# A cross network on one core: row products of the middle layers in 32x32 pieces instead of 32x128

## The chip, the cores and the metric

One NeuronCore of a Trainium2 chip runs the whole program. The metric is the device time of one execution in microseconds; the runs of the kernel before have a median of 131.04 us (130.76 to 131.1).

Names used below: PE is TensorE, which multiplies (PEld its weight loads), ACT is ScalarE, DVE is VectorE, POOL is GpSimd, SP the engine that issues most DMAs. SBUF is the memory on the core, PSUM the eight banks (each 512 fp32 wide on 128 partitions) into which PE writes.

## The reference

Six layers of a cross network on a batch of 4096 rows of 416 features, all in bf16:

```python
B, F, D, L = 4096, 26, 16, 6
Din = min(F * D, 1024)          # 416
...
def reference(x0, ws, bs):
    x = x0
    for l in range(ws.shape[0]):
        x = x0 * (x @ ws[l] + bs[l]) + x
    return x
```

## The kernel before

**Layout.** The activations are kept transposed: features on partitions, batch rows along the free dimension. 416 features are three chunks of 128 (tiles `XM`, main part) and a remainder of 32. The remainder has only 32 features, so four groups of 512 batch rows are put below each other on the 128 partitions (tile `XR`: partitions 32g to 32g+31 hold group g). The batch is cut in two halves s of 2048 columns, each in four groups g of 512 columns (`CW`). `WM` holds the weights of the 384 main input features, `WR` those of the 32 remainder features, once on each strip of 32 partitions, so that group g finds them beside its data. `XM` and `XR` each have three buffers: x0, and two that the layers use in turn.

**A middle layer** (the loop over `l` from 1 to 4) has six tiles (s, m): for a half s and an output chunk m of 128 features, all four groups. A tile fills two pairs of banks (`new_pts`), one bank for a group. Its product is the sum of two parts:

- `mm_full` (L205), for each group: over the three input chunks k, and for each k four products of 128 input rows x 32 output columns, side by side in the array by columns (position (0, 32q)); 48 products for a tile.
- `mm_row` (L211), once for a tile: for each group g one product of 32 input rows x 128 output columns, the four side by side in the array by rows (position (32g, 0)), each into the bank of its group; 4 products for a tile.

The tiles are taken in pairs (ta, tb). Within a pair the order is fixed by the program: the `mm_full` of ta in all groups, then `mm_row` of ta (which closes its sums), `mm_row` of tb (which opens its sums), then the `mm_full` of tb. So the two `mm_row` calls stand next to each other; such a place is called a visit below. There are 4 layers x 3 pairs = 12 visits of 8 products. After the first pair of a layer `rem_pair` makes the 32 remainder outputs, in products of 128x32 (L217, L222).

**Behind the products.** `ew_main` takes a pair of banks (half h of a tile): ACT adds the bias and writes bf16 (L169), DVE multiplies by x0 (L179) and adds the layer's input (L180). In `ew_rem` the same is done for the remainder (L193, L198, L199). The order of instructions on every engine is the order in which the program is written; semaphores between the engines are put in from the tiles that each instruction reads and writes.

**The first layer** uses products of 128x128 (L240) and 32x128 (L247). **The last layer** turns the roles around, so that its output has batch rows on partitions: products of 128x128 (L357) and 32x128 (L366, and L371 for the bias), then ACT copies (L383, L396), DVE multiplies (L384, L397) and adds (L385, L400), and SP sends the result out.

Of the kernel before, what the change touches and what calls it, by code (L numbers as in the profile page):

```python
# [16 lines left out]
def kernel(  # L17
# [7 lines left out]
    nc = tc.nc  # L25
# [8 lines left out]
    CW = 512  # L34
# [19 lines left out]
    WR = const.tile([P, L, D], BF16)  # L54
# [146 lines left out]
    def mm_full(l, s, m, g, pts, cur, first, last):  # L201
        c0 = col0(s, g)
        for k in range(NK):
            for q in range(4):
                nc.tensor.matmul(pts[g // 2][32 * q:32 * q + 32, g % 2, :], lhsT=WM[:, l, k, 128 * m + 32 * q:128 * m + 32 * q + 32],  # L205
                                 rhs=cur[:, k, c0:c0 + CW], start=(first and k == 0), stop=(last and k == NK - 1),
                                 tile_position=(0, 32 * q), skip_group_check=True)

    def mm_row(l, s, m, pts, curR, first, last):
        for g in range(NG):  # L210
            nc.tensor.matmul(pts[g // 2][:, g % 2, :], lhsT=WR[32 * g:32 * g + 32, l, 128 * m:128 * m + 128],  # L211
                             rhs=curR[32 * g:32 * g + 32, CW * s:CW * s + CW],
                             start=first, stop=last, tile_position=(32 * g, 0), skip_group_check=True)

    def mm_rem(l, s, pr, cur, curR):
        for g in range(NG):
# [97 lines left out]
    cur, curR = XM[1], XR[1]  # L314
    for l in range(1, LL):
        nxt, nxtR = XM[1 + (l % 2)], XR[1 + (l % 2)]
        feeds_last = (l == LL - 1)
        tiles = [(s, m) for s in range(NS) for m in range(NK)]
        pts = {}

        def finish(t):
            s, m = t
            for h in range(2):
                ew_main(l, s, m, h, pts[t][h], cur, nxt)
            if feeds_last:
                xl_dmat(s, m, nxt)

        for n in range(0, len(tiles), 2):
            ta, tb = tiles[n], tiles[n + 1]
            pts[ta] = new_pts()  # L330
            for g in range(NG):
                mm_full(l, ta[0], ta[1], g, pts[ta], cur, True, False)
            mm_row(l, ta[0], ta[1], pts[ta], curR, False, True)
            pts[tb] = new_pts()
            mm_row(l, tb[0], tb[1], pts[tb], curR, True, False)
            finish(ta)
            for g in range(NG):
                mm_full(l, tb[0], tb[1], g, pts[tb], cur, False, True)
            finish(tb)
            if n == 0:  # L340
                rem_pair(l, cur, curR, nxtR, feeds_last)
        cur, curR = nxt, nxtR

    l = LL
# [111 lines left out]
```

## Time and profile before

| what | value |
|---|---|
| median of three runs | 131.04 us |
| the profiled execution | 130.19 us |
| its span, first to last instruction | 128.1 us |
| granted TensorE clock | 1.000 |
| middle layers on PE (first to last visit) | 28.4 to 99.6 us |
| products of L205, L211, all on PE | 1152, 96, 1677 |

How to read it. A line of a group gives the source line, engine, operation, output <- inputs and shape, then the number of instructions, busy time in us, the mean of one in ns, and the idle time of the engine just before them with what ended it. For a matmul, 128*32 stands for input rows x output columns of the array; 128x512 is the streamed operand. A line of the order of time gives the start in us, the length of the stretch, and what ran in it; matmuls of one kind are put together. Matmuls are pipelined: the record of one lasts 379 ns where the next ones start earlier, so the distance between starts, not the length of a record, says how fast they go. A line of waits gives who waited for whom, the sum in us, how often, and the longest. "issue" is time in which the engine waited for nothing that the profile shows.

### The profile page before, as it was taken

To read this page: it belongs to the slowest core of one execution; us is meant where nothing else is said; L and a number is where in the kernel's file an instruction comes from. 1 tells how busy PE (TensorE), PEld (TensorE's weight loads), DVE (VectorE), ACT (ScalarE), POOL (GpSimd) and SP (SyncE) were. 2 spreads that over 40 slices of the span, in tenths; PEclk is the share of its full clock that TensorE was granted. 3 is DMA by queue.
4 is the path that set the end of the run, shared out by engine and by line. 5 is a ranking of instruction groups with operands and counts; after the bars stand their busy time and mean duration, and the time that the engine had idled before them with its cause. 6 is when DMAs were issued, how large, how long until landed. Compare 5 with 4: busy or idle time off the path is not lost. (4 is left out here: it accounts for less than half of the span.)

```text
span 128.1 us, 3929 instructions
## 1 busy us (share of the span) xinstructions
PE 122.7 (96%) x1677; PEld 54.7 (43%) x1677; DVE 105.2 (82%) x192; ACT 83.5 (65%) x94; POOL 8.6 (7%) x29
## 2 busy tenths in 40 slices
PE   6999999999999999999999999999999999999960
PEld 3344344444444444444444544444444445445420
DVE  3347959357979898989898989898989999999991
ACT  2117559489666849666849666749666777567860
POOL 4282000120000000000000000000000300000000
PEclk9999999999999999999999999999999999999999
DMA  3999999999990000000000000000398899986663
GB/s 91 259 157 192 207 187 263 229 329 332 336 314 24 5 0 8 0 0 5 0 5 0 5 0 5 0 0 5 69 140 177 167 122 246 192 283 216 210 225 103
DMA packets 42029, 16.36 MB, mean 128 GB/s; under 512 B 30838, under 2 KB 42012, under 8 KB 42012
## 3 DMA queue, kind: packets, MB, share of 16 engines
q1 hardware_dynamic: 40512, 15.70, 55.0%
q10 hardware_dynamic: 1500, 0.42, 1.6%
q8 instruction: 13, 0.21, 0.7%
q14 instruction: 4, 0.03, 0.1%
HBM read 6.15 MB, written 3.41 MB: 75 GB/s over the span
## 5 line engine op out<-in xcount | busy, mean ns | idle before, releaser
L169 ACT ACTIVATE t<-PS,bM 128x1024 bf16<-128x1024 f32 x56 | 58.1, 1115 | 21.2 <-PE PS L211 21.2
L205 PE MATMUL PS<-XM,WM 128*32 128x512 bf16 x1152 | 65.2, 379 | 0.0
L205 PEld LDWEIGHTS <-WM 128*32 128x32 bf16 x1152 | 29.8, 97 | 33.7 <-issue 5.1
L179 DVE TENSOR_TENSOR t<-t,XM 128x1024 bf16<-128x1024 bf16 x48 | 33.4, 695 | 4.1 <-ACT t L169 4.1
L180 DVE TENSOR_TENSOR XM<-t,XM 128x1024 bf16<-128x1024 bf16 x48 | 33.5, 699 | 3.1
L357 PE MATMUL PS<-WM,XM 128*128 128x416 bf16 x96 | 17.9, 340 | 0.0
L240 PE MATMUL PS<-XM,WM 128*128 128x512 bf16 x72 | 16.5, 383 | 0.1
L383 ACT CAST t<-PS 128x832 bf16<-128x832 f32 x12 | 10.2, 852 | 5.0 <-PE PS L357 2.5
L357 PEld LDWEIGHTS <-XM 128*128 128x128 bf16 x96 | 8.9, 98 | 8.7 <-issue 2.1
L240 PEld LDWEIGHTS <-WM 128*128 128x128 bf16 x72 | 6.9, 99 | 9.4 <-issue 2.1
L222 PE MATMUL PS<-XM,WM 128*32 128x512 bf16 x120 | 8.2, 379 | 0.0
L193 ACT ACTIVATE t<-PS,bR 128x512 bf16<-128x512 f32 x10 | 6.8, 694 | 1.9 <-POOL WD L133 1.9
L385 DVE TENSOR_TENSOR o<-t,XLrows 128x832 bf16<-128x832 bf16 x12 | 7.1, 592 | 0.5
L211 PE MATMUL PS<-XR,WR 32*128 32x512 bf16 x96 | 7.3, 379 | 0.0
L384 DVE TENSOR_TENSOR t<-t,X0rows 128x832 bf16<-128x832 bf16 x12 | 7.0, 586 | 0.0
L300 POOL COPY XLrows<-scrR 128x512 bf16<-128x512 bf16 x2 | 1.4, 698 | 72.7 <-DMA scrR<-XR 72.7
L177 DVE TENSOR_TENSOR XM<-t,XM 128x1024 bf16<-128x1024 bf16 x7 | 4.7, 690 | 1.5 <-ACT t L169 1.4
L150 PE MATMUL PS<-warm 128*128 128x512 bf16 (+2 forms) x13 | 4.6, 536 | 1.0 <-DVE warm L87 1.0
L186 ACT ACTIVATE t<-PS,bM 128x512 bf16<-128x512 f32 x4 | 2.6, 685 | 3.8 <-PE PS L247 3.8
L162 ACT COPY XR<-xrt 64x256 bf16<-64x256 bf16 x2 | 1.2, 621 | 5.7 <-DVE xrt L161 5.7
L161 DVE STREAM_TRANSPOSE xrt<-xrem 64x256 bf16<-64x256 bf16 (+1 forms) x5 | 2.2, 477 | 3.2 <-DMA xrem<-in_x_dram 3.2
L396 ACT CAST t<-PS 128x416 bf16<-128x416 f32 x8 | 4.0, 506 | 1.0 <-PE PS L357 0.8
(44 smaller groups left out, 54.4 us busy)
## 6 DMA issues: line engine op xcount, KB each, us to landing
X0rows<-in_x_dram SPq DMA_DIRECT2D x8, 416.0 KB, 7.5
WM<-in_ws_dram SPq DMA_DIRECT2D x5, 312.0 KB, 6.7
out_dram<-o SPq DMA_DIRECT2D x3, 416.0 KB, 3.2
out_dram<-o SPq DMA_DIRECT2D x6, 208.0 KB, 2.5
out_dram<-o SPq DMA_DIRECT2D x8, 104.0 KB, 1.7
WR<-in_ws_dram SPq DMA_DIRECT2D x4, 130.0 KB, 5.7
WM<-in_ws_dram ACTq DMA_DIRECT2D x1, 312.0 KB, 3.4
XM<-in_x_dram SPq DMA_TRANSPOSE x8, 4.8
```

Source lines behind the costliest of these rows:

```text
L169: nc.scalar.activation(t[:], pt.rearrange("p a b -> p (a b)"), ACT.Identity, bias=bM[:, m, l:l + 1], scale=1.0)
L179: nc.vector.tensor_tensor(out=t, in0=t, in1=x0c, op=ALU.mult)
L180: nc.vector.tensor_tensor(out=nxt[:, m, c0:c0 + 2 * CW], in0=t, in1=cur[:, m, c0:c0 + 2 * CW], op=ALU.add)
L193: nc.scalar.activation(tr[:, 0:CW], pr, ACT.Identity, bias=bR[:, l:l + 1], scale=1.0)
L205: nc.tensor.matmul(pts[g // 2][32 * q:32 * q + 32, g % 2, :], lhsT=WM[:, l, k, 128 * m + 32 * q:128 * m + 32 * q + 32], rhs=cur[:, k, c0:c ...
L211: nc.tensor.matmul(pts[g // 2][:, g % 2, :], lhsT=WR[32 * g:32 * g + 32, l, 128 * m:128 * m + 128], rhs=curR[32 * g:32 * g + 32, CW * s:CW ...
L222: nc.tensor.matmul(pr[32 * g:32 * g + 32, :], lhsT=WM[:, l, k, NK * P:D], rhs=cur[:, k, c0:c0 + CW], start=False, stop=(k == NK - 1), tile ...
L240: nc.tensor.matmul(pt[:, gl, :], lhsT=WM[:, 0, k, 128 * m:128 * m + 128], rhs=cur[:, k, c0:c0 + CW], start=(first and k == 0), stop=(last ...
L357: nc.tensor.matmul(py[g // 2][:, g % 2, 0:D], lhsT=cur[:, k, q_cols(q, g)], rhs=WM[:, l, k, :], start=(first and k == 0), stop=((not first ...
L383: nc.scalar.copy(tv, py[h][:, :, 0:D])
L384: nc.vector.tensor_tensor(out=tv, in0=tv, in1=X0rows[:, b0:b0 + 5:4, :], op=ALU.mult)
L385: nc.vector.tensor_tensor(out=o, in0=tv, in1=XLrows[:, b0:b0 + 5:4, :], op=ALU.add)
```

## The change

In `mm_row` each product of 32x128 is issued as four products of 32x32: the 128 output columns are cut into four strips q of 32, each with its own 32 columns of `WR`, its own 32 partitions of the bank, and the array position (32g, 32q). The data streamed, the bank and the accumulation flags are as before. A visit then has 32 products instead of 8.

```diff
     def mm_row(l, s, m, pts, curR, first, last):
         for g in range(NG):
-            nc.tensor.matmul(pts[g // 2][:, g % 2, :], lhsT=WR[32 * g:32 * g + 32, l, 128 * m:128 * m + 128],
-                             rhs=curR[32 * g:32 * g + 32, CW * s:CW * s + CW],
-                             start=first, stop=last, tile_position=(32 * g, 0), skip_group_check=True)
+            for q in range(4):
+                nc.tensor.matmul(pts[g // 2][32 * q:32 * q + 32, g % 2, :],
+                                 lhsT=WR[32 * g:32 * g + 32, l, 128 * m + 32 * q:128 * m + 32 * q + 32],
+                                 rhs=curR[32 * g:32 * g + 32, CW * s:CW * s + CW],
+                                 start=first, stop=last, tile_position=(32 * g, 32 * q), skip_group_check=True)
```

## The prediction

> **What bounds the kernel now.** I read the page's busy line first, then the waits, then the middle layers' order of time, and the vector engine (DVE) up to the end.
>
> ```profile
> PE 122.7 (96%) x1677; PEld 54.7 (43%) x1677; DVE 105.2 (82%) x192; ACT 83.5 (65%) x94; POOL 8.6 (7%) x29
> ...
> L205 PE MATMUL PS<-XM,WM 128*32 128x512 bf16 x1152 | 65.2, 379 | 0.0
> ...
> L211 PE MATMUL PS<-XR,WR 32*128 32x512 bf16 x96 | 7.3, 379 | 0.0
> ```
>
> The matmul rows have no idle time before them. Busy alone says little for pipelined matmuls, so the waits decide:
>
> ```profile
> ACT t L169 <- PE PS L211: 21.2, 12, 2.2
> ...
> PEld L211 <- issue: 5.1, 12, 0.4
> PEld L205 <- issue: 5.1, 12, 0.4
> DVE t L179 <- ACT t L169: 4.1, 11, 0.9
> ```
>
> ScalarE (ACT) waits at all twelve visits for the row products of L211, and DVE waits for ACT at eleven of them: in the middle layers TensorE (PE) sets the pace. The order of time of PE shows one period, in waves of products that run side by side:
>
> ```profile
> 36.00 0.61 PE L211 MATMUL PS<-XR,WR 32*128 32x512 bf16 x8
> 36.54 5.36 PE L205 MATMUL PS<-XM,WM 128*32 128x512 bf16 x96
> 41.84 0.61 PE L211 MATMUL PS<-XR,WR 32*128 32x512 bf16 x8
> 42.38 5.36 PE L205 MATMUL PS<-XM,WM 128*32 128x512 bf16 x96
> ```
>
> From 36.54 to 41.84 are 5.30 us for 24 waves of four 128x32 products. The records of single products inside it lie 0.2155 us apart from wave to wave, and 24 x 0.2155 = 5.17. The other 0.13 us, and what a visit costs beyond two waves, is seen at its borders:
>
> ```profile
> 35.68 0.39 PE L205 MATMUL PS<-XM,WM 128*32 128x512 bf16 x4
> 36.00 0.39 PE L211 MATMUL PS<-XR,WR 32*128 32x512 bf16 x4
> ...
> 36.01 0.60 PE L211 MATMUL PS<-XR,WR 32*128 32x512 bf16 x6
> ...
> 36.54 0.40 PE L205 MATMUL PS<-XM,WM 128*32 128x512 bf16 x4
> ...
> 36.00 0.12 PEld L211 LDWEIGHTS <-WR 32*128 32x128 bf16 x8 [0.42 <-issue]
> ```
>
> The last wave of 128x32 starts at 35.68, the first of 32x128 at 36.00: 0.32 instead of 0.2155, so going over costs about 0.10. The second row wave starts at 36.23, 0.227 after the first, the next 128x32 wave at 36.54, 0.31 later: another 0.10 back. The weight loads, elsewhere a wave ahead, wait these 0.42 us for "issue": nothing is loaded ahead across the border. A visit, 36.00 to 36.54, is 0.54 us.
>
> Last, the end. DVE's order of time shows its last wait:
>
> ```profile
> 94.64 0.43 DVE L199 TENSOR_TENSOR XR<-t,XR 128x512 bf16<-128x512 bf16 x1
> 95.29 0.69 DVE L179 TENSOR_TENSOR t<-t,XM 128x1024 bf16<-128x1024 bf16 x1 [0.22 <-ACT t L169]
> 96.01 0.69 DVE L180 TENSOR_TENSOR XM<-t,XM 128x1024 bf16<-128x1024 bf16 x1
> ```
>
> Behind 95.29 no wait of DVE is listed up to 125.1: the end hangs on DVE from there. That operation follows the eleventh visit (93.71). The twelfth (99.55) has room: ACT's output for it is ready at 101.1 (99.98 plus one activation of 1.115), DVE takes it up at 101.49. So what ten visits and the first wave of an eleventh gain or lose goes into the end.
>
> **The change, part by part.** Twelve visits (four layers, three pairs of tiles) have 96 products of 32x128; they become 384 of 32x32. PE gets 288 matmuls and 288 weight loads more, 1677 to 1965 each; nothing else changes kind, place or order, and no DMA is added.
>
> *Array time.* Four strips by rows, with 512 columns streamed, were one wave; four by rows and four by columns are still one wave of 512, if all sixteen run together. Each direction alone does it now: four column strips start within 0.011 us (L205 above, x4 in 0.39 with 0.379 each), four row strips too. Both at once is in no row. Lower bound 0; upper bound, if the column strips of a row strip took turns, 3 more waves of 0.2155 for each of two: 1.29 us a visit. I take 0: it is the product of two things that the rows show, and each pair of strips has its own partitions and each g its own bank (pts[g // 2], g % 2).
>
> *Issue.* The four row products of a wave start at 36.000, 36.003, 36.007 and 36.010, their loads between them: 3.4 ns per load and product. Sixteen spread over 15 x 3.4 = 51 ns instead of 10. A product of wave two follows the one of wave one on its own strip, so the spread is carried on, not doubled; and the next 128x32 wave waits for the last one to be out, as it does now (302 ns from the last record of the row wave, 36.236, to the first load at 36.538). That is 12 x 3.4 = 41 ns a visit: 0.58 instead of 0.54. It could be hidden only where the border did not wait for the last product, bound 0; the upper bound is the slowest pace at which PE is seen fed, four loads and products in 0.2155, 54 ns each. I take 3.4, the row of the same line and place. The Trainium skill (TensorE: Matmul & The Clock Gate, section "Measured speedup vs the span model") counts about 4 ns of issue per tile; by it the added spread is 48 ns a visit and the sum below 0.50 instead of 0.43, an estimate.
>
> *Weight loads.* Sixteen in place of four, each shorter in columns: 128x32 loads take 97 ns, 32x128 loads 92, so no shorter by these rows. The first sixteen lie in the spread already counted; the second sixteen need about 16 x 3.4 = 54 ns of issue, then 97, inside the 216 ns of wave one: 65 ns of cover. Without it each further pair costs its 3.4.
>
> *Borders.* 128x32 to 32x32 takes the place of 128x32 to 32x128. Rows of other changes of shape:
>
> ```profile
> 102.47 0.39 PE L205 MATMUL PS<-XM,WM 128*32 128x512 bf16 x4
> 102.79 0.35 PE L357 MATMUL PS<-WM,XM 128*128 128x416 bf16 x1
> ...
> 103.68 0.34 PE L357 MATMUL PS<-WM,XM 128*128 128x416 bf16 x1
> 103.95 0.35 PE L366 MATMUL PS<-WR,XR 32*128 32x416 bf16 x4
> ```
>
> Columns alone (128x32 to 128x128): 0.32 instead of 0.2155. Rows alone (128x128 to 32x128): 0.27 instead of 0.175 from product to product there. Both at once (L205 to L211): 0.32. All are 0.10 over a wave, so the new one, rows alone, is taken at the same 0.10: change 0. Bounds: minus 0.10 on each side, if it needs no emptying; plus nothing the rows suggest.
>
> *Semaphores.* ACT's first half needs the products of g 0 and 1: eight issues instead of two, 6 x 3.4 = 20 ns later in the visit. That is all of the eleventh visit that DVE sees.
>
> *Sum.* 10 x 41 + 20 = 430 ns. PE itself ends its middle layers 12 x 41 = 0.49 us later; the last 0.06 lies in the 0.4 us of room. The profiled execution took 130.19 us (span 128.1), which becomes 130.62; the runs' median is 131.04, 0.85 above it, and I put the sum on that: 131.47, said as 131.5.
>
> **Rivals.**
> *PE is not fed fast enough.* The 3.4 ns are seen for bursts of at most some dozen instructions (four loads with four products and four further loads at 36.00); a visit now wants 64 in a row. If loads and products come every r ns, the point is r = 215.5/16 = 13.5. Up to there the spread grows (15 r); beyond, first to last product of a visit takes 31 r, against 0.236 now. At 13.5 that is 0.42, +0.18 a visit, x 10.5 = +1.9: 132.9. At 54, the seen floor of supply, 1.67: +15.1, 146. For it: nothing in the rows shows a longer burst. Against: loads run a wave ahead in L205, so there are instructions waiting, and the 0.42 us at each border refill what stands ahead. I price it at 13.5, since that is the geometric middle of 3.4 and 54: 133. The same page of the Trainium skill (section "Wait — 56ns, not 53.3ns?") states a floor of about 25 ns from start to start however small a product is; applied to sixteen strips it would give 31 x 25 = 0.78 a visit and some 136.7, an estimate; the 3.4 ns between strips here speak against it.
>
> *Column strips of one row strip take turns* (the change doesn't do what it says): 1.29 us a visit, x 10.5 to 12 = 13.5 to 15.5, about 145. Against: both directions work alone.
>
> *The border gets cheaper, and the kernel faster.* The place is the two borders of a visit; the new form keeps the 32 columns of its neighbours, so PE may load ahead across it and need no emptying. Price: 2 x 0.10 saved, 0.04 of spread lost: minus 0.16 a visit, x 10.5 = minus 1.7: 129.3. It decides as soon as the two borders together fall by more than 41 ns. DVE would follow: it waits 4.1 us in all there. Against: rows alone and columns alone each cost the full 0.10 elsewhere.
>
> **How the numbers follow.** 0.3%, 0.39 us, is about what a measurement of this kernel can tell from no change. Forecast (+0.3 to +0.6) 0.62, of it two thirds over 0.39; too slow a supply 0.17; turns 0.05; a cheaper border 0.12; a spread that is hidden (131.0) 0.04. Slower: 0.41 + 0.17 + 0.05 = 0.63. Same: 0.21 + 0.04 = 0.25. Faster: 0.12. The range 130.9 to 133.2 holds the forecast, the hidden spread and the supply up to a little past its point; the cheaper border, the turns and a far slower supply are left out, 0.2 together. The forecast's own range is 131.3 to 131.7.
>
> **What would show it.** The row group reads 32*32, x384. Right: its first to second wave still about 0.23, each visit about 0.58 from the first row product to the next 128x32 wave, sixteen starts within about 0.05, borders of 0.32, DVE's last wait still behind the eleventh visit and some 0.4 us later. A visit of 0.7 or more with even gaps of over 13 ns is the supply; one of 1.8 with groups of four 0.2155 apart is turns; weight loads of L211 no longer waiting for "issue" and a visit under 0.5 is the cheaper border. I am wrong if the borders or the gap between strips in the combined form differ from the rows of the single forms.

## The result, and the profile after

The changed kernel takes 131.5 us (131.1 to 132.01, 14 runs), the kernel before, on the same chips, 131.18 us (130.57 to 131.44, 14 runs). The ratio is 1.003, with a 95% interval of 1.0018 to 1.0043: slower by 0.39 us, 0.24 to 0.56 (0.32 between the two medians). The prediction had 131.5 and +0.43.

The group of the row products, and the waits, on the page and in the list of waits of the changed kernel:

```profile
PE 123.8 (96%) x1965; PEld 55.8 (43%) x1965; DVE 105.2 (81%) x192; ACT 83.5 (64%) x94; POOL 9.2 (7%) x29
...
L213 PE MATMUL PS<-XR,WR 32*32 32x512 bf16 x384 | 7.8, 379 | 0.0
...
ACT t L169 <- PE PS L213: 21.7, 12, 2.3
PEld L213 <- issue: 5.1, 12, 0.4
PEld L205 <- issue: 4.6, 12, 0.4
```

384 products of 32x32 take 7.8 us of busy time, where 96 of 32x128 took 7.3. The weight loads still wait 0.4 us for "issue" at each of the twelve visits: nothing is loaded ahead across the border. The order of time of PE around one visit:

```profile
36.54 0.39 PE L205 MATMUL PS<-XM,WM 128*32 128x512 bf16 x4
36.86 0.43 PE L213 MATMUL PS<-XR,WR 32*32 32x512 bf16 x16
...
37.09 0.42 PE L213 MATMUL PS<-XR,WR 32*32 32x512 bf16 x16
37.44 0.40 PE L205 MATMUL PS<-XM,WM 128*32 128x512 bf16 x4
...
36.86 0.20 PEld L213 LDWEIGHTS <-WR 32*32 32x32 bf16 x32 [0.42 <-issue]
```

Sixteen products start within 0.43 minus 0.384 (one record) = 0.05 us; the second wave starts 0.23 behind the first; the visit, 36.86 to 37.44, is 0.58. The single records give more digits. Over the twelve visits the mean is 0.5806 against 0.5404. The way in, from the last main product to the first row product, is 0.309 (before 0.312), the way out 0.304 (0.304).

The spans of the two profiled executions differ by more, 129.5 against 128.1. Most of that is not the change: the first visit starts at 29.26 instead of 28.44, and nothing ahead of it was edited. The eight kernels below, which share this unedited first layer, begin their first visit between 28.74 and 29.32. From the first visit to the last instruction it is 100.22 against 99.70: 0.52.

### The profile page after: what moved, and what is told of

It reads as the page before. It is cut to its first block, busy times and chain, and to the rows that moved or that the text cites. A ratio compares the mean times of both kernels' runs of the same rounds, so it can differ in the third digit from the quotient of the medians.

```text
span 129.5 us, 4505 instructions
## 1 busy us (share of the span) xinstructions
PE 123.8 (96%) x1965; PEld 55.8 (43%) x1965; DVE 105.2 (81%) x192; ACT 83.5 (64%) x94; POOL 9.2 (7%) x29
## 4 chain that ended last, share of the span: by engine, by line
PE 75%; SPq 10%; DVE 6%; DMA 5%; issue 1%; ACT 1%; DVEq 0%
PE PS L205 49%; SPq L77 9%; PE PS L360 8%; PE PS L213 5%; PE PS L225 5%; DMA XM<-in_x_dram 5%; PE PS L243 3%; PE PS L220 2%; DVE t L400 2%; DVE o L403 1%; DVE o L388 1%; DVE t L387 1%; PE PS L369 1%; SPq L82 1%; PE PS L374 1%
## 5 line engine op out<-in xcount | busy, mean ns | idle before, releaser
L243 PE MATMUL PS<-XM,WM 128*128 128x512 bf16 x72 | 17.0, 389 | 0.1
L213 PE MATMUL PS<-XR,WR 32*32 32x512 bf16 x384 | 7.8, 379 | 0.0
L303 POOL COPY XLrows<-scrR 128x512 bf16<-128x512 bf16 x2 | 2.0, 1013 | 73.3 <-DMA scrR<-XR 73.3
```

What stands on the lines that cost most here:

```text
L243: nc.tensor.matmul(pt[:, gl, :], lhsT=WM[:, 0, k, 128 * m:128 * m + 128], rhs=cur[:, k, c0:c0 + CW], start=(first and k == 0), stop=(last ...
```

## The experiments

Each row wave belongs to a call of `mm_row`; a visit has two, the closing one of tile ta and the opening one of tb. A median of before is that of the kernel before, run beside it on the same chip.

**Half the pieces.** The edit, in the kernel before:

```diff
-            nc.tensor.matmul(pts[g // 2][:, g % 2, :], lhsT=WR[32 * g:32 * g + 32, l, 128 * m:128 * m + 128],
+            for q in range(2):
+                nc.tensor.matmul(pts[g // 2][64 * q:64 * q + 64, g % 2, :],
+                                 lhsT=WR[32 * g:32 * g + 32, l, 128 * m + 64 * q:128 * m + 64 * q + 64],
...
-                             start=first, stop=last, tile_position=(32 * g, 0), skip_group_check=True)
+                                 start=first, stop=last, tile_position=(32 * g, 64 * q), skip_group_check=True)
```

> The row products are cut in two pieces of 32x64 instead of four of 32x32, 16 products a visit instead of 8 (before) or 32 (changed). Issue spread: each added load and product costs 3.3 to 3.4 ns once per visit, 4 x 3.35 = 13 ns, so a visit takes 0.553 us (0.540 before, 0.580 changed) and the borders stay at 0.31 from the last product to the next load. Rival, the cost belongs to going over to pieces of another column width: a visit of 0.58, as with 32x32.

The visit takes 0.568, between the two expectations (0.553 and 0.58): the expectation missed a term. The loads and products come 3.3 ns apart, so eight starts spread over 23 ns instead of 10: that is the 13 expected. The other 14 were not. They lie between the first wave and the second, 0.240 instead of 0.226. The loads by form, of the changed kernel and of this one, suggest why:

```profile
L213 PEld LDWEIGHTS <-WR 32*32 32x32 bf16 x384 | 2.4, 88 | 5.1 <-issue 5.1
```

```profile
L212 PEld LDWEIGHTS <-WR 32*64 32x64 bf16 x192 | 1.9, 102 | 5.1 <-issue 5.1
```

A load of 64 columns takes 102 ns, one of 32 columns 88, and one of 128 columns took 91 to 92 before: its record in the trace alone shows the columns read in four parts of 32. Directly behind a border the load is not hidden (42.765, its product 42.766), and 14 ns more of load stand beside 14 ns more of visit. That the load is the cause is argued from these equal numbers; no run changes the load alone. So the cost is not proportional to the pieces alone; in the 32x32 form the load is the shortest of the three, and the spread is all that is left. (Time: 131.4 us in a single run, median of before 130.58; too coarse for 0.2 us.)

**More products in the same wave.** The changed kernel with each product cut along the streamed columns, here into two of 256, and in the next one into four of 128:

```diff
+        for c in range(0, CW, NC):
             for g in range(NG):
                 for q in range(4):
-                    nc.tensor.matmul(pts[g // 2][32 * q:32 * q + 32, g % 2, :],
+                    nc.tensor.matmul(pts[g // 2][32 * q:32 * q + 32, g % 2, c:c + NC],
...
-                                     rhs=curR[32 * g:32 * g + 32, CW * s:CW * s + CW],
+                                     rhs=curR[32 * g:32 * g + 32, CW * s + c:CW * s + c + NC],
-                                     start=first, stop=last,
+                                     start=(first and c == 0), stop=(last and c + NC == CW),
```

> The changed kernel, with each 32x32 product of 512 columns issued as two of 256 columns, 64 products and 64 loads a visit. If loads and products keep coming every 3.3 ns, four rounds of sixteen strips take 0.108 each, the spread is still 0.05, and a visit stays at 0.57 to 0.60: within 0.2 us of the changed kernel. If the supply is slower than 6.7 ns for a load and product, the visit grows as 63 r + 0.2: 1.05 us at r = 13.5, which is 5.6 us more in the whole.

> As before, in pieces of 128 columns: 128 products and 128 loads a visit, sixteen strips of 54 ns each, so issue every 3.35 ns is just enough. Issue spread alone: 127 x 3.35 + 0.14 = 0.57, up to 0.62 for a visit, within 0.5 us of the changed kernel. Supply at 13.5 ns: 1.85 a visit, +15 us. Supply at 25 ns: 3.3 a visit, +33 us. The even gap between products in the trace gives r by itself.

Measured: 135.74 us with 256 columns (median of before 130.58; ratio 1.0366, 1.0299 to 1.0432) and 150.7 with 128 (its quickest run 147.96). The trace with 256 columns, PE in order of time:

```profile
37.61 2.12 PE L205 MATMUL PS<-XM,WM 128*32 128x512 bf16 x33
41.44 3.63 PE L205 MATMUL PS<-XM,WM 128*32 128x512 bf16 x62 [1.71 <-issue]
45.00 0.88 PE L215 MATMUL PS<-XR,WR 32*32 32x256 bf16 x64
...
45.00 0.44 PE L215 MATMUL PS<-XR,WR 32*32 32x256 bf16 x32
...
45.30 0.57 PE L215 MATMUL PS<-XR,WR 32*32 32x256 bf16 x32
45.81 0.40 PE L205 MATMUL PS<-XM,WM 128*32 128x512 bf16 x4
```

and with 128 columns:

```profile
49.08 1.32 PE L215 MATMUL PS<-XR,WR 32*32 32x128 bf16 x128
50.33 5.36 PE L205 MATMUL PS<-XM,WM 128*32 128x512 bf16 x96
```

The visit is 0.81 and 1.25 instead of 0.58. Both lie between the two expectations, 0.60 and 1.05 with 256 columns, 0.62 and 1.85 with 128: issue every 3.3 ns does not last, but r is below 13.5. In the single records of the visit at 45.00 the first 32 loads (to 45.100) and 32 products (to 45.168), 64 instructions, come at that pace; then nothing but one load starts for 0.135 us. Part of that is the array: a strip needs half of 0.2155, 0.108 us, for 256 columns, so the third wave, due 0.108 behind 45.118, is 0.08 late. From 45.303 on loads and products alternate, one pair every 8.3 ns: 45.311, 45.319, 45.328, 45.336 for four products in a row. With 128 columns it is the same: a gap from 55.737 to 55.871, and 8.3 ns behind it. (That kernel's granted clock was 0.972 in the mean; the gaps are read where it was full.) These 8.3 ns are the r that the prediction left open. They lie under the point of 13.5, so sixteen strips of 512 columns would be fed even without a stock (16 x 8.3 = 133 of 215.5 ns, worked out and not run); strips of 256 (16 x 8.3 against 108) and of 128 (against 54) are not. The changed kernel's visit has just 64 instructions. Its last two loads are 8 ns apart (36.960, 36.968), all before 3.3. So it seems to stand at the end of the stock, and the 0.30 us of the border behind it are long enough for a gap like the 0.135 above.

The kernel with 256 columns pays 12 x 0.268 = 3.2 us in its visits against before, and 2.1 from 37.61 to 45.00, a stretch that takes 5.29 in the next pair; for 1.71 of it, up to 41.44, PE stands and waits for nothing that the profile shows. The DMA engines are full until shortly before (share 0.93 from 38 to 39, 0.04 from 40 to 41), and a 16 KB packet of the instruction queue runs from 38.94 to 40.06. Late instructions are one guess; PE stands on for 1.4 us behind that packet, and no run here settles the cause.

**One form in each half of a visit.** The closing wave in 32x32, the opening one in 32x128:

```diff
-            mm_row(l, tb[0], tb[1], pts[tb], curR, True, False)
+            mm_row_wide(l, tb[0], tb[1], pts[tb], curR, True, False)
```

> In each visit the closing products are 32x32 and the opening ones stay 32x128. If every change of shape empties the array (0.308 from the last product to the next load), a visit is 0.051 + 0.308 + 0.012 + 0.302 = 0.67, 0.13 more than before, and twelve of them give +1.5 us against the kernel before. Rival, the emptying belongs only to going over between 128 and 32 input rows: a visit of about 0.56 and +0.2 us.

132.44 us, median of before 130.58, ratio 1.0148 (1.0123 to 1.0172), that is +1.6 to +2.25. PE in order of time:

```profile
42.63 0.43 PE L213 MATMUL PS<-XR,WR 32*32 32x512 bf16 x16
42.99 0.40 PE L220 MATMUL PS<-XR,WR 32*128 32x512 bf16 x4
43.32 5.36 PE L205 MATMUL PS<-XM,WM 128*32 128x512 bf16 x96
```

From 42.63 to 43.32 is 0.69. The border between two forms of 32 rows that differ in columns alone costs as much as any other (0.317 from the last 32x32 to the first 32x128 product); the rival falls. The 0.02 over the expectation are mostly the 10 ns longer first wave behind a border, now there twice, which the expectation had left out.

**Where the delay goes.** The kernel before, with the opening wave issued five times in one single visit, the last of twelve (shown) or the sixth (`(2, 4)` in place of `(LL - 1, 4)`). Each wave restarts its sums:

```diff
+            for rep in range(5 if (l, n) == (LL - 1, 4) else 1):
-            mm_row(l, tb[0], tb[1], pts[tb], curR, True, False)
+                mm_row(l, tb[0], tb[1], pts[tb], curR, True, False)
```

> The kernel before, with the opening row wave (four products, sums restarted each time) issued five times instead of once, in the twelfth visit alone: 4 x 0.2155 = 0.86 us more on TensorE, nothing else. As the prediction has it (VectorE sets the end from 95.29 on, the twelfth visit has room): 0 to +0.45 us. Rival, TensorE and VectorE run level in the last layer (ScalarE's copy at 116.34 ends at 117.19, VectorE takes it up at 117.22, only 0.03 to 0.1 us of room): +0.75 to +0.85 us, and VectorE waits for a copy in the last layer.

> The same 0.86 us of added TensorE time in the sixth visit (second middle layer, third pair). Both: +0.75 to +0.86 us, since VectorE waits behind later visits. If it is less, a delay in the middle layers is partly made up and the sum of the prediction passes through too much.

Last visit: 131.7 against 130.54, ratio 1.0075 (1.0048 to 1.0102), +0.63 to +1.33. Sixth visit: 131.52 against 130.54, ratio 1.0063 (1.0041 to 1.0086), +0.54 to +1.12. From the first visit to the last instruction both are 100.55 against 99.70 before: +0.85 each. So of the 0.86 added in the last visit 0.85 arrive at the end; the room that the prediction gave it is not there. DVE in order of time in the last layer, before:

```profile
116.70 0.59 DVE L385 TENSOR_TENSOR o<-t,XLrows 128x832 bf16<-128x832 bf16 x1
117.22 0.59 DVE L384 TENSOR_TENSOR t<-t,X0rows 128x832 bf16<-128x832 bf16 x1
```

and with the long last visit:

```profile
116.52 0.59 DVE L386 TENSOR_TENSOR o<-t,XLrows 128x832 bf16<-128x832 bf16 x1
117.44 0.59 DVE L385 TENSOR_TENSOR t<-t,X0rows 128x832 bf16<-128x832 bf16 x1 [0.33 <-ACT t L384]
118.12 0.59 DVE L386 TENSOR_TENSOR o<-t,XLrows 128x832 bf16<-128x832 bf16 x1
118.77 0.59 DVE L385 TENSOR_TENSOR t<-t,X0rows 128x832 bf16<-128x832 bf16 x1
```

Now DVE waits for ACT's copies, and those for PE. The multiply at 118.77 is the one at 117.22 before; counted from each run's first visit it is 0.84 later.

**The suspected cost paid twice.** The opening wave is moved behind the first group's main products, so that a visit becomes two; once with 32x128, once with 32x32:

```diff
-            mm_row(l, tb[0], tb[1], pts[tb], curR, True, False)
+            mm_full(l, tb[0], tb[1], 0, pts[tb], cur, True, False)
+            mm_row(l, tb[0], tb[1], pts[tb], curR, True, False, (0,))
             finish(ta)
-            for g in range(NG):
+            for g in range(1, NG):
                 mm_full(l, tb[0], tb[1], g, pts[tb], cur, False, True)
```

(The last argument makes group 0 close its sum in `mm_row` instead of opening it.)

> The kernel before (32x128 products), with the opening row wave of a pair moved behind the first group's main products, so that each visit becomes two of one wave each: 24 visits, 48 borders instead of 24. Each added pair of borders costs the 0.20 us that the trace of before shows (0.10 on each side), less nothing, plus some 0.01 for the first main wave behind each border: +0.20 to 0.22 per pair of tiles, twelve of them: +2.4 to +2.6 us against the kernel before. If the borders were hidden work: 0.

> The same with 32x32 products, so that the suspected cost of the change is paid twice as often: the spread of sixteen starts, 12 x 3.4 = 41 ns, once in each of 24 visits. Theory (spread per visit, all on the path): 0.9 to 1.0 us over the other kernel of this call, twice what the change costs in the kernel before. Rival, the cost hangs on the number of products or of instructions fetched (the same 384 as in the changed kernel): 0.3 to 0.5 us over the other kernel.

Wide: 133.48 against 131.27, ratio 1.0185 (1.0157 to 1.0212), +2.1 to +2.8. Narrow: 134.36, ratio 1.0248 (1.0223 to 1.0273). The two differ by 0.88 us in the medians, 0.895 from first visit to last instruction, just under the 0.9 to 1.0 expected, where the change itself shows 0.52; no interval was taken for the pair alone. PE in order of time, wide and then narrow:

```profile
43.01 0.40 PE L212 MATMUL PS<-XR,WR 32*128 32x512 bf16 x4
43.33 0.83 PE L205 MATMUL PS<-XM,WM 128*32 128x512 bf16 x12
44.09 0.40 PE L212 MATMUL PS<-XR,WR 32*128 32x512 bf16 x4
```

```profile
43.08 0.43 PE L214 MATMUL PS<-XR,WR 32*32 32x512 bf16 x16
43.45 0.83 PE L205 MATMUL PS<-XM,WM 128*32 128x512 bf16 x12
44.20 0.43 PE L214 MATMUL PS<-XR,WR 32*32 32x512 bf16 x16
```

Each visit is 0.365 instead of 0.325 in the mean of 24: 0.040 again, 24 times. The narrow kernel has 288 products more than the wide one, as the changed kernel has over the one before, so a cost by product or by fetched instruction would have stayed at 0.3 to 0.5. It doubled with the visits: from the first visit to the last PE takes 75.54 us against 74.69, 0.85 more, where the change shows 0.41.

## Why the prediction was right

*Array time: right.* Sixteen strips run together, 16 products in 0.43, and the next wave 0.23 later.

*Issue: right, and its size too.* 41 ns a visit were predicted, 40.2 measured. The pace within the wave is 3.3 ns. (At 4 ns the prediction's own sum is 10 x 48 + 24 = 504 ns, so just over 0.50 and not below.) The second sixteen loads, which come without products between them, are 3.3 ns apart as well (36.913 to 36.946), so the loads alone may set this pace; no run separates it. The way in is 2.7 ns shorter, which leaves 37.5; between the first and the last visit PE takes 71.52 instead of 71.11 us, 0.41 over eleven visits.

*Weight loads: right that they are covered*, though the cover is thinner. The last of the second sixteen starts at 36.968 and takes 87 ns, to 37.055; the second wave starts at 37.087. 32 ns are left of the 65 predicted, as the second sixteen start only behind the first wave's spread. (That load's own product is the last of its wave, at 37.137, and has 82.)

*Borders: right.* 0.309 and 0.304, and the mixed kernel shows the same between two row forms. The rival of the cheaper border falls.

*The way to the end: wrong in its reason.* "So what ten visits and the first wave of an eleventh gain or lose goes into the end" failed: the prediction read from the missing waits of DVE behind 95.29 that the twelfth visit "has room". In the last layer ACT's tenth copy, which waits for PE, says otherwise:

```profile
116.34 0.85 ACT L383 CAST t<-PS 128x832 bf16<-128x832 f32 x1 [0.48 <-PE PS L357]
```

It ends at 117.19, and DVE takes it up at 117.22. The 0.03 us between are no room: from the end of this copy to the take-up it is 0.032 or 0.033 us in all ten kernels here, also with the long last visit and in the kernels with two visits for a pair, where DVE has to wait. So DVE is held by this copy already before the change, for about 0.015 us (524 ns from the addition to this multiply, 508 to 510 at the ten others like it), which its list of waits does not show. PE's pace is what puts the copy there. The room of 0.4 at 101.49 is real, but it is used up fifteen microseconds later. The sign that the prediction had named, DVE's last listed wait still behind the eleventh visit and 0.4 later, came true all the same (96.54 in the changed kernel) and could not tell the two apart.

By this way twelve visits at 37.5 ns give 0.45, and the 20 ns for ACT's first half drop out; by the prediction's way it was 0.43. A pace taken 3.5 ns too high and a visit and a half left out nearly cancel, and that is luck. In the changed kernel the chain that ended last shows it directly:

```profile
115.61 0.46 PE PS L369 x8
116.08 0.35 PE PS L374 x8
116.43 1.18 PE PS L360 x6
...
117.62 0.86 ACT t L386
...
118.51 0.60 DVE t L387
```

It runs along PE through all middle layers and into the last layer, and changes to ACT and DVE only at 117.62. The take-up at 118.51 is, from the first visit, 0.46 us later than before. The other 0.06 of the 0.52 arise behind it, in work that the change does not touch and that takes between 10.90 and 10.98 us in the ten kernels (10.91 before, 10.97 changed).

*Too slow a supply: its mechanism exists, its price here is nothing.* The rival's 13.5 ns was the right point to look at; the measured 8.3 stays below it. The changed kernel's own visit, 0.58, shows nothing of it. The Trainium skill (TensorE: Matmul & The Clock Gate, the table at its head) gives PE's queue 64 entries, which agrees with the 64 instructions that come at 3.3 ns before the pace falls. Its floor of about 25 ns from start to start ("Wait — 56ns, not 53.3ns?") does not hold between different strips, where these runs show 3.3 and 8.3.

*Strips taking turns* fell with the first point.

## What to carry to other kernels

Cutting a product that already fills the array together with its neighbours gains nothing, and costs the issue of the added pieces once at each place where the array must run empty; count the places, not the products. A list of waits without an entry is not room: look for the smallest distance between a result and its use along the rest of the run, and compare it with the same distance where a wait is certain; here 0.03 us was the handover itself, and no room at all. A profiled span of one run can differ by 0.8 us ahead of any edit; compare from the first edited place on.

## What the runs showed of the hardware

- A change of shape costs the same 0.09 to 0.10 us beyond the wave, whether rows, columns or both change: 0.309 and 0.304 with 32x32 (rows), 0.312 and 0.304 with 32x128 (both), 0.317 from 32x32 to 32x128 (columns, with the 10 ns of a first wave behind a border in it). Two more such borders per pair of tiles cost +2.1 to +2.8 us over twelve pairs.
- A load and product come every 3.3 ns for 64 instructions; then no product started for 0.135 us, and it went on at 8.3 ns for a load and product (products of 256 and of 128 columns).
- The load of a 32x64 piece is slower (102 ns) than that of 32x128 (91 to 92) and of 32x32 (88), and behind a border the first wave with it lasts 14 ns longer (0.240 against 0.226).
- From the end of ACT's tenth copy of the last layer to DVE's take-up it is 0.032 to 0.033 us in all ten kernels, whether a wait is listed or not.
